# Loading two tokens of a head side by side, and splitting them by token parity, in a gated linear attention + MLP kernel

## The chip, the cores and the metric

The kernel runs on one core of one Trainium2 chip. The metric is the device time of one execution in microseconds; several runs without a profile give a median. One further execution is recorded by the hardware profiler; the views quoted below are of that execution. TensorE appears in them as PE (matmuls) and PEld (weight loads), VectorE as DVE, ScalarE as ACT, GpSimd as POOL, SyncE as SP. A `q` after an engine's name means its queue of instructions, where DMAs are issued.

## The reference

Four tensors `q`, `k`, `v`, `f_logit` of shape (4 batches, 8 heads, 768 tokens, 48) go through a gated recurrence for each batch and head, and the result, laid out as (4, 768, 384), goes through a LayerNorm and a two-layer MLP with a residual:

```python
f = 1 / (1 + exp(-f_logit))
for t in range(S):
    state = f[:, :, t, :, None] * state + einsum('bhd,bhe->bhde', k[:, :, t], v[:, :, t])
    y[:, :, t] = einsum('bhd,bhde->bhe', q[:, :, t], state)
x = y.transpose(0, 2, 1, 3).reshape(B, S, H * D)
xn = (x - mean) / sqrt(var + 1e-6) * g_ln
out = x + maximum(xn @ w_ch1, 0) @ w_ch2       # 384 -> 1536 -> 384
```

## The kernel before

The 768 tokens are cut into 12 units of 64 tokens, each of all four batches, so a unit is 256 rows of the MLP. `attention(n)` has the stages of unit n's recurrence (gates, two scans along the tokens, scores, values, state), and `mlp(n)` its two layers. From unit 3 on the first layer runs as 15 products of blocks (`by_blocks`, lines 916 to 979) and the second, from unit 2 on, as seven (`product` inside `mlp`, L1025). All matmuls are in float32.

The order of all work is written out by hand. `START` (lines 302 to 318) and `UNIT` (319 to 325) are lists of tokens that `run` (1075) turns into instructions: `a3.k` is the stage `k` of unit 3, `m2` the next step of unit 2's MLP, `l5k` a load of k for unit 5 from SP's queue and `L5k` from ACT's, `p4q0` the split number 0 of q for unit 4 with its write on POOL's queue and `P4q1` number 1 with its write on SP's, `x4k` the transpose of k for unit 4, which SP issues. Each engine and each queue works through its instructions in this order, so an instruction that waits holds what stands behind it. The transposes, the output and most of the loads share SP's queue.

For the recurrence, f, q and k are needed with the feature of a head on the partitions and the tokens along the free dimension, while DRAM has them with the features innermost. Units 0 to 2 (`n < DIRECT`) are transposed by TensorE in `across` (646). Units 3 to 11 go another way[...]:

- `load` (455) fills a tile `[128, G, H, 64]` (G = 2, H = 8). Batch b of a unit has 64 tokens; they lie on the partitions (b % 2) * 64 to + 64, in the half g = b // 2 of the tile. Each token of a head is 48 floats, 192 B, followed by 16 columns of filling. One load is one batch: 64 partitions x 8 heads, 512 runs of 192 B. Four loads make one tensor of a unit.
- `split` (425) takes one half g of the tile (two batches) and has ACT copy it into a tile `planes` that holds the low and the high 2-byte words apart (L433). There are two such buffers, used in turn by all tensors. Then a DMA writes `planes` into a DRAM tile (L437), 256 runs of 1 KB.
- `transfer` and `transposed` (439, 449) turn both halves in one DMA transpose (L452) of 256 rows by 1,024 two-byte columns, 8 blocks of 128 columns. Low and high words of a value land side by side, so the tile can be read as float32: `turned` for f and q, `qraw` for k.

From unit 3 on, q is loaded into the raw tile of k (`raw_of`, 414), which shows as `kraw<-in_q_dram` in the profile. The gated key `kh` goes the same way once more, with the name K: it is split (`Kplanes`), written and transposed into `kt` (stage `kt`, 768), which the state update uses.

In `attention`, a pair of heads of one of the two halves g is numbered by e, 0 to 7; `pairs` (617) lists them with g outermost. `do_kept` (721) scales the state by the unit's total gates, `do_values` (782) copies the result of the recurrence out of PSUM into `x`.

The filling is 40.0 for f, so that its gate is 1, and 0.0 for q and k (401 to 403). The smallest product of gates is kept in `least`, and at the end a flag decides whether a slower path must redo the work (L1118 to L1128, 1132).

Of the kernel before, what the change touches and what calls it, by code (L numbers as in the profile page):

```python
# [12 lines left out]
U16 = mybir.dt.uint16  # L13
AF = mybir.ActivationFunctionType
ALU = mybir.AluOpType
# [313 lines left out]
def kernel(  # L329
# [38 lines left out]
    DIRECT = 3  # L368
    HALVED = 1
    PIECE = 768  # L370

    outer = ctx.enter_context(tc.tile_pool(name="outer", bufs=1))
    ident = outer.tile([P, P], FP32)
# [8 lines left out]
    raws = fast.enter_context(tc.tile_pool(name="raws", bufs=2))  # L382
# [11 lines left out]
    def one_bank(name):  # L394
        return ps1.tile([P, 512], FP32, tag="one", name=name)
# [2 lines left out]


    wide_heads = {}  # L400
    for name, fill in (("f", 40.0), ("q", 0.0), ("k", 0.0)):
        t = consts.tile([P, G, H, 64], FP32, name=f"{name}raw")
        nc.gpsimd.memset(t[:, :, :, D:64], fill)
        wide_heads[name] = t
    loaded = {}

# [13 lines left out]
    def whole(n, name):  # L420
        if name != "K":
            return raw_of(n, name)
        return by_gates[n].rearrange("p (g s) t -> p g s t", g=G)

    def split(n, name, g, queue):

        if n >= NU or n < DIRECT:
            return
        if (n, name) not in halved:
            halved[n, name] = drams.tile([P, 2, G, 64 * H], U16, tag=f"{name}halves",  # L430
                                         name=f"{name}halves{n}")
        planes = raws.tile([P, 2, 64 * H], U16, tag="planes", name=f"{name}planes{n}_{g}")
        nc.scalar.copy(  # L433
            out=planes,
            in_=whole(n, name)[:, g].rearrange("p h e -> p (h e)").bitcast(U16).rearrange(
                "p (c two) -> p two c", two=2))
        queue.dma_start(out=halved[n, name][:, :, g], in_=planes)  # L437

    def transfer(n, name):

        if n >= NU or n < DIRECT:
            return
        if not turned:
            turned["k"] = wide_heads["q"].rearrange("p g h e -> p (g h e)").rearrange(
                "p (s t) -> p s t", t=T)
            turned["f"] = turned["q"] = work.tile([P, NS, T], FP32, name="turned")
        transposed(turned[name].rearrange("p (g s) t -> p g (s t)", g=G), n, name)

    def transposed(dst, n, name):
        there = halved.pop((n, name))  # L450
        to = dst.rearrange("p g c -> p (g c)").bitcast(U16)
        nc.sync.dma_start_transpose(out=to.rearrange("p (a r) -> p a r", a=GA),  # L452
                                    in_=there.rearrange("p two g c -> (p two) (g c)"))

    def load(n, name, gs=range(B // 2), engines=(nc.sync,)):
        if n >= NU:
            return
        if name != "v":
            loaded[n, name] = raw_of(n, name)
        elif (n, name) not in loaded:  # L460
            loaded[n, name] = raws.tile([P, G, H, D], FP32, tag="rawv", name=f"v{n}")
        src = {"f": f_logit, "k": k, "q": q, "v": v}[name]
        for b in (b for b in range(B) if b // 2 in gs):
            engines[b % len(engines)].dma_start(  # L464
                out=loaded[n, name][(b % 2) * T:(b % 2 + 1) * T, b // 2, :, 0:D],
                in_=src[b, :, n * T:(n + 1) * T, :].rearrange("h p d -> p h d"))

    load(0, "f", (0,), (nc.sync, nc.scalar))

    power = consts.tile([P, 2], FP32)  # L470
# [24 lines left out]
    state = consts.tile([P, 2, GA, D], FP32)  # L495
# [118 lines left out]

    pairs = [(g, a) for g in range(G) for a in range(NP)]
# [8 lines left out]
    def attention(n):  # L626

        both = range(G)
        gt = gates
# [13 lines left out]
        def of(gs):  # L643
            return [ega for ega in enumerate(pairs) if ega[1][0] in gs]
# [75 lines left out]

        def do_kept():

            if n:
                nc.vector.tensor_tensor(
                    out=new("kept", [P, 2, GA, D]), in0=state, op=ALU.mult,
                    in1=at["total"].rearrange("p (e b) -> p b e", b=2).unsqueeze(3).broadcast_to(
                        [P, 2, GA, D]))

        def do_carried():

# [37 lines left out]
        def do_kt():  # L768

            kt, kh = new("kt", [P, GA, P]), at["kh"]  # L770
            if n >= DIRECT:
                transposed(kt.rearrange("p (g a) c -> p g (a c)", g=G), n, "K")
                return
            for g in range(G):
                pt = one_bank(f"kp{n}").rearrange("p (a c) -> p a c", a=NP)
                for a in range(NP):
                    e = g * NP + a
                    nc.tensor.transpose(
                        pt[:, a], kh[:, 2 * e:2 * e + 2].rearrange("p b t -> p (b t)"), ident)
                nc.scalar.copy(out=kt[:, g * NP:(g + 1) * NP], in_=pt)  # L780

        def do_values(gs=both):
            py, sc, vt = at["py"], at["sc"], loaded[n, "v"]
            for e, (g, a) in of(gs):
# [12 lines left out]
            for b in range(2):  # L797
                nc.scalar.copy(out=xv[half(b), 1, gsl], in_=pyv[half(1 - b), 1, gsl])
# [276 lines left out]
    def run(plan):  # L1075
        for token in plan.split():
            kind, rest = token[0], token[1:]
            if kind == "a":
# [3 lines left out]
                if "a" + n not in running:  # L1082
                    running["a" + n] = attention(int(n))
# [32 lines left out]
    for m in range(3, NU):  # L1116
        run(UNIT.format(m=m, n=m + 1, o=m + 2, p=m + 3, z=m + 4))
        if m == NU - 3:  # L1118
            worst = consts.tile([P, 1], FP32)
            nc.vector.tensor_reduce(out=worst, in_=least, axis=mybir.AxisListType.X, op=ALU.min)  # L1120
        if m == NU - 2:
            pw = one_bank("pw")
            nc.tensor.transpose(pw[0:1, 0:P], worst, ident)
            least_one = consts.tile([1, 1], FP32)
            nc.vector.tensor_reduce(out=least_one, in_=pw[0:1, 0:P], axis=mybir.AxisListType.X,
                                    op=ALU.min)
            nc.vector.tensor_scalar(out=small, in0=least_one, scalar1=LEAST, scalar2=None,
                                    op0=ALU.is_lt)  # L1128
# [37 lines left out]
```

## Time and profile before

| What | us |
|---|---|
| median of 3 runs without a profile | 442.06 (441.48 to 442.35) |
| the profiled execution, its own time | 445.22 |
| its span, first to last instruction | 443.2 |
| DVE, ACT, POOL busy | 332.1, 215.5, 111.2 |

The span is 2.0 us shorter than the profiled execution's own time. In the middle of the run a unit takes about 33 us: the second-layer products of units 6, 7, 8 and 9 begin at 231.95, 266.22, 300.29 and 333.22 us. In the profile's names, L464 is any load, L433 a copy of a split, L437 its write, L452 a transpose, L1038 the output; a line is that of the helper, so it is the tile's name that tells which tensor is meant. A matmul's end is modelled, and a wait for several semaphores is put down to the one that came last.

### The profile page before, as it was taken

The page shows a single profiled execution, that of the slowest core. Times are in us where ns is not written, and L with a number is a line of the kernel's source. Part 1 is how long each engine was busy: PE and PEld are TensorE (multiplying, and loading weights), DVE is VectorE, ACT ScalarE, POOL GpSimd, SP SyncE. Part 2 cuts the span into 40 slices and gives each one's busy share as a digit, 9 for nine tenths or more (in the row PEclk, how much of TensorE's full clock was granted, in tenths as well). Part 3 has the DMA queues.
Part 4 walks back from the last instruction along what each step waited for, and adds up shares of the span by engine and source line. Part 5 has one row for each costly group of instructions (what it writes and reads, how often), then busy time and mean ns, then how long its engine had stood idle before and what let it go on. Part 6 is the DMA issues. An engine that isn't in the chain of part 4 may idle for free.

```text
span 443.2 us, 12936 instructions
## 1 busy us (share of the span) xinstructions
PE 422.5 (95%) x5435; PEld 392.0 (88%) x5435; DVE 332.1 (75%) x538; ACT 215.5 (49%) x364; POOL 111.2 (25%) x136
## 2 busy tenths in 40 slices
PE   6889998999999999999989999998999999999995
PEld 4678885667889999989979999989999999999995
DVE  5998676578856888788777798787798798567361
ACT  2665655444543573663554465456366443160320
POOL 2352334831023115014013114014114003002011
PEclk9999999999999999999998999999999999999999
DMA  9999898987897896899798798799787780400101
GB/s 166 274 232 226 173 229 215 190 150 192 163 206 170 210 202 169 164 186 200 161 187 197 176 188 176 188 174 201 179 184 188 180 157 10 123 1 10 29 5 36
DMA packets 200270, 71.68 MB, mean 162 GB/s; under 512 B 179408, under 2 KB 194000, under 8 KB 200208
## 3 DMA queue, kind: packets, MB, share of 16 engines
q1 hardware_dynamic: 176992, 57.27, 64.5%
q0 software_dynamic: 2960, 9.70, 6.3%
q10 hardware_dynamic: 20256, 3.84, 5.5%
q8 instruction: 44, 0.72, 0.7%
q14 instruction: 18, 0.15, 0.1%
HBM read 28.31 MB, written 23.59 MB: 117 GB/s over the span
## 4 chain that ended last, share of the span: by engine, by line
PE 64%; SPq 12%; DMA 11%; ACT 5%; issue 5%; DVE 1%; POOL 1%; ACTq 0%; POOLq 0%; DVEq 0%
PE pp L1025 28%; PE po L1006 7%; PE bx L931 7%; DMA kraw<-in_k_dram 6%; SPq L464 6%; PE by L931 5%; SPq L1038 3%; PE ph L996 2%; DMA qraw<-in_q_dram 2%; PE py L738 2%; PE ph L880 2%; PE bv L931 2%; PE shared L752 2%; PE bz L931 2%; PE bw L931 2%
## 5 line engine op out<-in xcount | busy, mean ns | idle before, releaser
L1025 PE MATMUL pp<-w,h 128*128 128x192 f32 x240 | 43.0, 337 | 5.1 <-ACT h L942 5.0
L1025 PEld LDWEIGHTS pp<-w,h 128*128 128x128 f32 x240 | 40.5, 196 | 6.2 <-ACT h L942 6.0
L942 ACT ACTIVATE h<-h 128x512 f32<-128x512 f32 x45 | 27.7, 627 | 35.6 <-DVE h L939 29.5
L1025 PE MATMUL pp<-mixed,h 128*128 128x192 f32 x240 | 42.3, 326 | 0.0
L1025 PE MATMUL pp<-mixed,s 128*128 128x192 f32 x240 | 40.6, 326 | 0.0
L1025 PEld LDWEIGHTS pp<-mixed,h 128*128 128x128 f32 x240 | 39.6, 190 | 0.3
L1025 PEld LDWEIGHTS pp<-mixed,s 128*128 128x128 f32 x240 | 39.3, 190 | 0.0
L433 ACT COPY kplanes<-kraw 128x1024 uint16<-128x1024 uint16 x18 | 18.9, 1051 | 32.4 <-DMA kraw<-in_k_dram 20.1
L1006 PE MATMUL po<-w,h 128*128 128x384 f32 x96 | 32.5, 490 | 1.8 <-ACT h L998 1.8
L658 DVE TENSOR_TENSOR_SCAN after<-gates,ends 128x1040 f32<-128x1040 f32 (+1 forms) x13 | 29.8, 2291 | 3.1 <-ACT gates L689 3.1
L433 ACT COPY Kplanes<-kh 128x1024 uint16<-128x1024 uint16 x18 | 18.3, 1050 | 28.3 <-DVE kh L706 16.5
L996 PE MATMUL ph<-xt,w 128*128 128x256 f32 x144 | 31.9, 381 | 0.0
L996 PEld LDWEIGHTS ph<-xt,w 128*128 128x128 f32 x144 | 27.2, 190 | 4.3 <-ACT xt L868 0.2
L939 DVE TENSOR_TENSOR h<-h,by 128x512 f32<-128x512 f32 x36 | 24.7, 687 | 8.0 <-PE by L931 3.2
L1006 PEld LDWEIGHTS po<-w,h 128*128 128x128 f32 x96 | 17.8, 190 | 13.3 <-issue 2.2
L931 PE MATMUL bx<-y,v 128*128 128x128 f32 x216 | 29.4, 279 | 0.0
L670 DVE TENSOR_TENSOR_SCAN upto<-gates,starts 128x1040 f32<-128x1040 f32 (+1 forms) x13 | 28.1, 2158 | 0.5
L1033 POOL TENSOR_TENSOR p1x<-p,x 128x192 f32<-128x192 f32 x10 | 10.7, 1066 | 67.0 <-ACT p L1040 67.0
L931 PEld LDWEIGHTS bx<-y,v 128*128 128x128 f32 x216 | 26.2, 192 | 0.5
L758 DVE TENSOR_TENSOR sc<-shared,causal 128x1024 f32<-128x1024 f32 x11 | 13.5, 1224 | 15.1 <-PE shared L752 15.1
L939 DVE TENSOR_TENSOR h<-h,bx 128x512 f32<-128x512 f32 x27 | 18.3, 677 | 8.4 <-PE bx L931 8.4
L813 POOL TENSOR_SCALAR rstd<-mv 128x2 f32<-128x2 f32 (+1 forms) x13 | 3.3, 250 | 82.6 <-DVE mv L811 82.4
(169 smaller groups left out, 952.9 us busy)
## 6 DMA issues: line engine op xcount, KB each, us to landing
w_0words<-in_moe_w_ch_dram SPq DMA_DIRECT2D x7, 768.0 KB, 6.4
v<-in_v_dram SPq DMA_DIRECT2D x46, 96.0 KB, 4.2
kraw<-in_k_dram SPq DMA_DIRECT2D x40, 96.0 KB, 4.4
fhalves<-fplanes SPq DMA_DIRECT2D x14, 256.0 KB, 2.6
khalves<-kplanes POOLq DMA_DIRECT2D x14, 256.0 KB, 4.7
kraw<-in_q_dram SPq DMA_DIRECT2D x36, 96.0 KB, 3.3
fraw<-in_f_logit_dram ACTq DMA_DIRECT2D x27, 96.0 KB, 3.6
Khalves<-Kplanes POOLq DMA_DIRECT2D x10, 256.0 KB, 3.4
```

The lines of the kernel that those rows point to most:

```text
L433: nc.scalar.copy(out=planes, in_=whole(n, name)[:, g].rearrange("p h e -> p (h e)").bitcast(U16).rearrange("p (c two) -> p two c", two=2))
L464: engines[b % len(engines)].dma_start(out=loaded[n, name][(b % 2) * T:(b % 2 + 1) * T, b // 2, :, 0:D], in_=src[b, :, n * T:(n + 1) * T, : ...
L658: nc.vector.tensor_tensor_scan(out=at["after"].rearrange(flat)[:, c0:c1][:, ::-1], data0=gt[:, c0 + 1:c1 + 1][:, ::-1], data1=ends.rearran ...
L670: nc.vector.tensor_tensor_scan(out=at["upto"].rearrange(flat)[:, c0:c1], data0=gt[:, c0:c1], data1=starts.rearrange(flat)[:, c0:c1], initi ...
L758: nc.vector.tensor_tensor(out=sc.rearrange("s r e t -> s (r e) t"), in0=at["ps"].rearrange("s r e t -> s (r e) t"), in1=causal.unsqueeze(1 ...
L931: nc.tensor.matmul(banks[bank][:, i], lhsT=right[:, i * P:(i + 1) * P], rhs=left, start=new and i == 0, stop=True, skip_group_check=True)
L939: nc.vector.tensor_tensor(out=out[to], in0=out[to], in1=bank, op=op)
L942: nc.scalar.activation(out=out[to], in_=out[to] if bank is None else bank, func=AF.Relu)
L996: nc.tensor.matmul(ph[:, j], lhsT=w1[:, m, (i + j) * P:(i + j + 1) * P], rhs=xt[:, m], start=m == 0, stop=m == KD - 1)
L1006: nc.tensor.matmul(po, lhsT=h[:, i, g * P:(g + 1) * P], rhs=w2[:, i], start=i == 0, stop=i == KF - 1)
L1025: nc.tensor.matmul(pp, lhsT=a[:, i], rhs=b[:, i], start=i == 0, stop=i == KH - 1)
L1038: engine.dma_start(out=out[2 * g + b, n * T:(n + 1) * T, cols], in_=o[half(b)])
```

## The change

From unit 3 on, a load puts two neighbouring tokens of a head side by side on one partition (R = 2). Batch b now lies on the partitions b * 32 to + 32, and a partition holds 8 heads x 96 floats without filling: one load has 256 runs of 384 B. A split takes the tokens of one parity i of all four batches: for each head 64 floats from column h * 96 + i * 48, so the 16 columns after the 48 are those of a neighbouring token or head instead of filling. The two parities are the two halves in the DRAM tile, whose runs become 2 KB, and the transpose of f, q and k has 512 rows and 4 blocks of 128 columns. K keeps its own shape.

With that the segments of a unit come out in another order, heads outside and batches inside (`by_heads`), so the state is reordered once, in `do_kept` of unit 3, and the copies to `x` read PSUM in the new order. The filling of f is 0.0, and the last minimum is taken over the 48 real rows of each 64 only. Units 0 to 2, `START` and `UNIT` stay as they are.

```diff
@@ def split @@
-            halved[n, name] = drams.tile([P, 2, G, 64 * H], U16, tag=f"{name}halves",
+            halved[n, name] = drams.tile([P, 2, 2, 64 * H], U16, tag=f"{name}halves",
...
-        nc.scalar.copy(
-            out=planes,
-            in_=whole(n, name)[:, g].rearrange("p h e -> p (h e)").bitcast(U16).rearrange(
-                "p (c two) -> p two c", two=2))
-        queue.dma_start(out=halved[n, name][:, :, g], in_=planes)
+        if name == "K":
+            src = by_gates[n].rearrange("p (i s) t -> p i (s t)", i=2)[:, i].bitcast(U16).rearrange(
+                "p (c two) -> p two c", two=2)
+            to, there = planes, halved[n, name][:, :, i]
+        else:
+            src = raw_of(n, name).rearrange("p g h e -> p (g h e)")[
+                :, i * D:i * D + (H - 1) * R * D + 64]
+            src = bass.AP(tensor=src.tensor, offset=src.offset,
+                          ap=[src.ap[0], [R * D, H], [1, 64]]).bitcast(U16).rearrange(
+                              "p h (c two) -> p two h c", two=2)
+            to, there = planes.rearrange("p two (h c) -> p two h c", h=H), halved[n, name][:, i]
+        nc.scalar.copy(out=to, in_=src)
+        queue.dma_start(out=there, in_=planes)
@@ def transfer, transposed @@
-        transposed(turned[name].rearrange("p (g s) t -> p g (s t)", g=G), n, name)
+        transposed(turned[name].rearrange("p s t -> p (s t)"), NP,
+                   halved.pop((n, name)).rearrange("p i two c -> (p i two) c"))
...
+    def transposed(dst, blocks, there):
+        nc.sync.dma_start_transpose(
+            out=dst.bitcast(U16).rearrange("p (a r) -> p a r", a=blocks), in_=there)
@@ def load @@
-            engines[b % len(engines)].dma_start(
-                out=loaded[n, name][(b % 2) * T:(b % 2 + 1) * T, b // 2, :, 0:D],
-                in_=src[b, :, n * T:(n + 1) * T, :].rearrange("h p d -> p h d"))
+            to = loaded[n, name]
+            if name == "v" or n < DIRECT:
+                to = to[(b % 2) * T:(b % 2 + 1) * T, b // 2, :, 0:D]
+                rows = src[b, :, n * T:(n + 1) * T, :].rearrange("h p d -> p h d")
+            else:
+                to = to.rearrange("p g h e -> p (g h e)")[
+                    b * T // R:(b + 1) * T // R, 0:H * R * D].rearrange("p (h c) -> p h c", h=H)
+                rows = src[b, :, n * T:(n + 1) * T, :].rearrange("h (p i) d -> p h (i d)", i=R)
+            engines[b % len(engines)].dma_start(out=to, in_=rows)
@@ def do_kept @@
+            for b in range(2):
                 nc.vector.tensor_tensor(
-                    out=new("kept", [P, 2, GA, D]), in0=state, op=ALU.mult,
...
+                    out=kept[:, b].rearrange("p (a g) d -> p a g d", g=G),
+                    in0=state[:, b].rearrange("p (g a) d -> p a g d", g=G), op=ALU.mult,
...
@@ def do_values @@
-            pyv = py[:, :, 0:GA * D].rearrange("t r (g a d) -> t r g a d", g=G, d=D)
+            pyv = py[:, :, 0:GA * D].rearrange(f"t r ({order} d) -> t r g a d", g=G, d=D)
```

More of the change, by code (lines that the diff above doesn't have):

```diff
@@ L370 @@
     PIECE = 768
+    R = 2
     outer = ctx.enter_context(tc.tile_pool(name="outer", bufs=1))
@@ L400 @@
     wide_heads = {}
-    for name, fill in (("f", 40.0), ("q", 0.0), ("k", 0.0)):
+    for name in "fqk":
         t = consts.tile([P, G, H, 64], FP32, name=f"{name}raw")
-        nc.gpsimd.memset(t[:, :, :, D:64], fill)
+        nc.gpsimd.memset(t[:, :, :, D:64], 0.0)
         wide_heads[name] = t
@@ L418, with split @@
     by_gates = {}
[L420 to L425, printed above, removed]
+    def split(n, name, i, queue):
         if n >= NU or n < DIRECT:
@@ L429, in split @@
         if (n, name) not in halved:
-            halved[n, name] = drams.tile([P, 2, G, 64 * H], U16, tag=f"{name}halves",
+            halved[n, name] = drams.tile([P, 2, 2, 64 * H], U16, tag=f"{name}halves",
                                          name=f"{name}halves{n}")
-        planes = raws.tile([P, 2, 64 * H], U16, tag="planes", name=f"{name}planes{n}_{g}")
-        nc.scalar.copy(
-            out=planes,
-            in_=whole(n, name)[:, g].rearrange("p h e -> p (h e)").bitcast(U16).rearrange(
-                "p (c two) -> p two c", two=2))
-        queue.dma_start(out=halved[n, name][:, :, g], in_=planes)
+        planes = raws.tile([P, 2, 64 * H], U16, tag="planes", name=f"{name}planes{n}_{i}")
+        if name == "K":
[11 more added lines that the diff above has]
+        queue.dma_start(out=there, in_=planes)
     def transfer(n, name):
@@ L446, in transfer @@
             turned["f"] = turned["q"] = work.tile([P, NS, T], FP32, name="turned")
-        transposed(turned[name].rearrange("p (g s) t -> p g (s t)", g=G), n, name)
[L449 to L453, printed above, removed]
+        transposed(turned[name].rearrange("p s t -> p (s t)"), NP,
[3 more added lines that the diff above has]
+            out=dst.bitcast(U16).rearrange("p (a r) -> p a r", a=blocks), in_=there)
     def load(n, name, gs=range(B // 2), engines=(nc.sync,)):
@@ L613, in mix_step @@
         late["steps"].send(engine)
-    pairs = [(g, a) for g in range(G) for a in range(NP)]
+    by_batch = [(g, a) for g in range(G) for a in range(NP)]
+    by_heads = [(g, a) for a in range(NP) for g in range(G)]
     x_of, norm_of, xn_of, xt_of, y_of, h_of, sums_of = {}, {}, {}, {}, {}, {}, {}
@@ L628, in attention @@
         both = range(G)
+        pairs, order = (by_batch, "g a") if n < DIRECT else (by_heads, "a g")
         gt = gates
@@ L721, in do_kept @@
         def do_kept():
-            if n:
+            if not n:
+                return
+            kept = new("kept", [P, 2, GA, D])
+            by = at["total"].rearrange("p (e b) -> p b e", b=2)
+            if n != DIRECT:
+                nc.vector.tensor_tensor(out=kept, in0=state, op=ALU.mult,
+                                        in1=by.unsqueeze(3).broadcast_to([P, 2, GA, D]))
+                return
+            for b in range(2):
                 nc.vector.tensor_tensor(
-                    out=new("kept", [P, 2, GA, D]), in0=state, op=ALU.mult,
-                    in1=at["total"].rearrange("p (e b) -> p b e", b=2).unsqueeze(3).broadcast_to(
-                        [P, 2, GA, D]))
+                    out=kept[:, b].rearrange("p (a g) d -> p a g d", g=G),
+                    in0=state[:, b].rearrange("p (g a) d -> p a g d", g=G), op=ALU.mult,
+                    in1=by[:, b].rearrange("p (a g) -> p a g", g=G).unsqueeze(3).broadcast_to(
+                        [P, NP, G, D]))
         def do_carried():
@@ L771, in do_kt @@
             if n >= DIRECT:
-                transposed(kt.rearrange("p (g a) c -> p g (a c)", g=G), n, "K")
+                transposed(kt.rearrange("p e c -> p (e c)"), GA,
+                           halved.pop((n, "K")).rearrange("p two i c -> (p two) (i c)"))
                 return
@@ L1123 @@
             nc.tensor.transpose(pw[0:1, 0:P], worst, ident)
+            of_heads = pw[0:1, 0:P].rearrange("o (r e) -> o r e", r=2)[:, :, 0:D]
             least_one = consts.tile([1, 1], FP32)
-            nc.vector.tensor_reduce(out=least_one, in_=pw[0:1, 0:P], axis=mybir.AxisListType.X,
+            nc.vector.tensor_reduce(out=least_one, in_=of_heads, axis=mybir.AxisListType.XY,
                                     op=ALU.min)
```

## The prediction, made before the changed kernel was run

> **What bounds the kernel now.** I began with the page: the engine shares, then the slices.
>
> ```profile
> span 443.2 us, 12936 instructions
> PE 422.5 (95%) x5435; PEld 392.0 (88%) x5435; DVE 332.1 (75%) x538; ACT 215.5 (49%) x364; POOL 111.2 (25%) x136
> DMA  9999898987897896899798798799787780400101
> ```
>
> TensorE is busy for 422.5 of 443.2 us. The change takes no matmul away, so all that it can win lies in the 20.7 us of TensorE's idle time. The third line says that the DMA engines are nearly full until late in the run. Next, the table of waits, of which these are the lines that touch the change:
>
> ```profile
> ACT kplanes L433 <- DMA kraw<-in_k_dram: 20.1, 8, 4.4
> ACT gates L685 <- DMA turned<-fhalves: 11.3, 6, 2.7
> ACT qplanes L433 <- DMA Khalves<-Kplanes: 7.6, 5, 2.2
> PE pp L1025 <- ACT h L942: 5.0, 4, 2.0
> ACT qplanes L433 <- DMA kraw<-in_q_dram: 2.2, 2, 1.1
> PE po L1006 <- ACT h L998: 1.8, 1, 1.8
> PE shared L825 <- DMA kt<-Khalves: 0.9, 1, 0.9
> ```
>
> Columns: total us, times, longest. Only the three PE lines cost time directly: 5.0 + 1.8 + 0.9 = 7.7 us. The first, four stalls, comes from ACT's order. The timeline by engine of one such stall (SP, then ACT, then PE; start, duration, what, and in brackets the idle time before and its cause):
>
> ```profile
> 221.30 1.08 SPq L437 DMA_DIRECT2D qhalves<-qplanes  x1
> 222.43 3.56 SPq L464 DMA_DIRECT2D kraw<-in_k_dram  x4
> ...
> 229.32 1.05 ACT L433 COPY kplanes<-kraw 128x1024 uint16<-128x1024 uint16 x1 [4.03 <-DMA kraw<-in_k_dram]
> 230.27 1.14 ACT L942 ACTIVATE h<-h 128x512 f32<-128x512 f32 x2
> ...
> 231.95 2.48 PE L1025 MATMUL pp<-w,h 128*128 128x192 f32 x7 [2.05 <-ACT h L942]
> ```
>
> Four loads of k are issued over 3.56 us, the last lands 3.2 us later (225.99 to 229.2), ACT sits in front of the copy for 4.03 us, the two Relus queue behind it, and the first matmul of the second MLP product waits 2.05 us. The same picture stands at 197.32 (1.02 us), 300.29 (1.63) and 333.22 (0.35): together 5.05 us.
>
> In the chain of waits the queue of SP is on the path too (SPq 12%, DMA 11%): between 174 and 191 us it issues without a real pause, and steps that take 0.57 us elsewhere take 1.05 (L437 at 186.99), four loads 3.46 instead of 2.63 to 2.78. I read those stretches as a queue that is held back by the backlog of descriptors. Last, the DMA queues:
>
> ```profile
> q1 hardware_dynamic: 176992, 57.27, 64.5%
> q0 software_dynamic: 2960, 9.70, 6.3%
> q10 hardware_dynamic: 20256, 3.84, 5.5%
> ```
>
> q10 is ACT's queue. Its packets can be counted: 37 loads (27 f, 8 k, 2 v) of 512 runs of 192 B = 18,944, of 20,256. They took 5.5% of 16 x 443.2 = 390 us, so 19.3 ns each. q0 (POOL's 37 writes of 256 KB, 64 packets of 4 KB and 16 small ones each) took 447 us, about 185 ns for 4 KB or 46 ns for 1 KB.
>
> **What the Trainium skill says.** *DMA: Bandwidth & Descriptors*, "Specifications", gives 512 B as the least size for full rate; the trace agrees in kind: 192 B in 19.3 ns is 10 B/ns, 4 KB in 185 ns is 22 B/ns. The same page, "How a descriptor splits into AXI transactions", says that a read that starts off a 256 B boundary fetches from the boundary below. Rows of 192 B then cost 6, 12, 10 and 8 beats in turn, 36 for four tokens; runs of 384 B cost 12 and 16, 28. This is an estimate from the page; no view shows beats. "Issuing engines are not separate DMA queues" on that page: moving a load between queues saves no engine time. Here q1, q10 and q0 do fill the same 16 engines. *ScalarE: Activation LUTs*, "What ACT_TABLE_LOAD costs", prices an instruction with immediate operands at 186 ns and 0.833 ns per element of a lane, whatever the function; 186 + 853 = 1.04 us for 1024 elements, and the trace has 1.04 us for the copies of all four tensors.
>
> **The change, part by part.** (1) Loads. For units 3 to 11, 9 x 3 x 4 = 108 loads have 256 runs of 384 B for 512 of 192 B: 27,648 packets less. A 384 B packet is in no row. Bounds: 19.3 ns (size free) and 38.5 ns (size everything, nothing saved). The line through 192 B and 1 KB gives 19.3 + 192 x (46 - 19.3)/832 = 25.5 ns, which I take. One load then needs 256 x 25.5 = 6,530 instead of 9,880 engine-ns, 0.21 us less on 16 engines (bounds 0 and 0.31); four loads 0.84 us, the twelve of a unit 2.5 us in about 34.
>
> (2) Writes of the halves for f, q, k: 2 KB runs for 1 KB on the SP queue (27 of them, 128 packets less each). By the same line 2 KB costs about 90 ns against 2 x 46: nothing, at most a tenth of a us each.
>
> (3) Splits. Same count and size of copies on ACT, now with rows of 64 instead of one run of 512. I take 1.04 us as before (bounds: no reason for less; if each row cost 10 ns more, 0.16 us each, hidden except where ACT is late). But each split now needs all four loads, and not the two of its half. For k in the steady part nothing changes: k1 is split first, and its half came with the last two loads. For q it does: q0 is split first, and its two loads were the early ones. What is queued behind q0 on ACT is q1, and q1 has another wait, for the buffer that the K write frees: it started 0.99, 1.62, 2.07 and 2.16 us after q0's end (at 184.05, 218.32, 286.31, 320.83). So q0 may be late by that much and nothing moves. Its last load is issued until 180.03 in the first of these units and may land 2.97 us later. With (1) I expect 2.2 to 2.6. Hidden. At 62.12 (first split of k, unit 3) and 89.64 (unit 4) two more loads are awaited too; half the packets pay for them.
>
> (4) Transposes of f, q, k as 512 rows x 4 blocks instead of 256 x 8. The count of packets in q1 leaves 2,064 per transpose, so 2,048 of 256 B: the same in both shapes. SP is held 1.3 to 4.4 us now, by backlog I think. I take no change of their own; bounds -0.5 and +1 us each. ACT's gates wait for f in six units, but the copies after them have 0 to 2.8 us of idle time and four PSUM banks in front of TensorE, so +1 us stays hidden.
>
> (5) DVE: the scaling of the state in unit 3 in two halves instead of one of 0.95 us; about 0.1 us once, on an engine with idle time. Memsets, the last minimum, the copies out of PSUM in another order: nothing.
>
> **The sum.** How much sooner does k come? The four issues shrink from 3.46-3.65 to about 2.7 us (0.8 to 0.9), their own packets drain 0.84 us sooner, and the stretched steps ahead (L1038, L437, about 0.5 us) shrink in part: 1.6 to 2.2 us. That removes 1.02, 1.63 and 0.35 whole and about 1.8 of 2.05: 4.8 us. In units without a stall (249 to 266 us) TensorE is busy for all 17.00 us, so the next limit is TensorE. The wait of 0.9 for kt (two transposes of 3.50 and 4.35 us behind loads of f and k) goes: 0.85. The wait of 1.84 at 72.18 comes from the second k split at 68.91, behind the write of fplanes and a backlog of loads and weights; two tensors' loads are 8 x 0.21 = 1.7 us less engine time. I take 1.0. Together 6.65 us; I leave 0.6 for stalls that come back smaller. So about -6.05. Against the profiled execution: 445.22 (span 443.2 and 2.0 around it) to 439.2. The median of the runs without a profile is 442.06, 3.2 lower; I assume the same stalls there: **436.0 us**.
>
> **Rivals.** *Most of the price is bytes.* If 384 B costs near 38 ns, only the issues shrink (256 KB writes with 256 runs take 0.57, loads with 512 take 0.65: 0.3 us per four) and some backlog: 0.5 us in four stalls, 2 us: 440.0. For it: GB/s in the slices stays at 150 to 250. Against: 19.3 ns for 192 B.
> *Nothing:* what the loads give, waits on planes buffers and on SP's order take; 442. Against: the k copies wait on no buffer in the four stalls.
> *Slower: the wait for the fourth q load.* If loads land no sooner, the last after 3.67 us as k's did at 293.89, q0 ends 0.7 us after q1 could have started in all four units (180.03 + 3.67 = 183.70 against 183.00; 0.7 each in the others). q1, its write on SP and the loads of k behind that slip by as much, and four stalls grow by 0.7: 442.06 + 2.9 = 445. It decides from 2.97 us between issue and landing. For it: ACT waited for q already in two units, with only two loads awaited. Against: fewer packets, and unstretched issues.
>
> **Chances and range.** Forecast (434.5 to 438.5) 0.63; mostly bytes 0.15; nothing 0.05; slower 0.17. Changes under 0.2%, 0.9 us, can't be told from none. Faster 0.78, same 0.05, slower 0.17. The range ends at the full 7.7 us with a little for the clock (434.0) and at 442.0, where the slower case is left out.
>
> **What would show it.** Right: about 169,200 packets in all (200,270 - 27,648 - 3,456), DMA share lower in the middle slices, four k loads in about 2.7 us on SP, ACT's wait for k under 10 us of 20.1, PE's for L942 under 1 us, q0 later but q1 still behind the K write. Wrong: transposes that take longer on SP; the q0 copy ending after the K write lands; or PE's idle time gone while the span stays, which would mean a lower clock or longer matmuls. What would make me wrong is above all a landing time that hangs on something other than packets.

## The result, and the profile after

| | before | after |
|---|---|---|
| median of 20 runs each, us | 442.1 (440.89 to 445.24) | 445.65 (441.52 to 452.74) |
| the profiled execution, us | 445.22 | 446.89 |
| its span, us | 443.2 | 444.9 |
| first block product (`bw`) of unit 3, the first full unit, us | 145.2 | 152.1 |
| the same of unit 11, eight units later, us | 410.9 | 412.6 |

The changed kernel is slower: ratio 1.0063, 95% interval 1.0038 to 1.0088, where 436.0 us had been forecast. (Ratios leave disturbed runs out, medians keep them, so the two can differ by a few tenths of a per cent.)

The last two rows of the table say where to look. (The expectations below call the first of these marks the second-layer product of the first full unit. The second-layer products begin with unit 2's at 127.95, so the one at 231.95 us is that of unit 5, and the four starts listed in "Time and profile before" belong to units 5 to 8.) Eight full units take 265.7 us before and 260.5 after: there the change gains 5.2 in these two executions. What comes ahead of the first full unit takes 6.9 us longer. A gain and a larger loss, in different stages. First the page of the changed kernel: granted clock and DMA share in slices, and ACT's queue.

```profile
PEclk9999999779999999999999999999999999999999
DMA  9999897662798887997989987897896790400101
...
q10 hardware_dynamic: 12064, 3.84, 4.3%
```

Two digits of the granted clock fall to 7: slices of 11 us, the eighth and ninth, from 78 to 100 us. In the same slices the DMA engines are at 6 and 6, where before has 9 and 8. Then the waits (total us, times, longest).

```profile
ACT kplanes L440 <- DMA kraw<-in_k_dram: 9.4, 6, 3.0
...
PE kp L799 <- DVE x L1032: 4.2, 1, 4.2
...
ACT gates L696 <- DMA turned<-fhalves: 3.0, 5, 1.4
```

TensorE's four waits for ACT in front of the second layer (5.0 us before) have no line left, and ACT's wait for k fell from 20.1 to 9.4, that for f (gates) from 11.3 to 3.0. New is one wait of TensorE for DVE, 4.2 us at one place. The timeline of TensorE (start, duration, what, and in brackets the idle time before) shows what follows from it:

```profile
69.56 10.84 PE L1027 MATMUL po<-w,h 128*128 128x384 f32 x32
84.59 1.97 PE L799 MATMUL kp<-ident,kh 128*128 128x128 f32 x8 [4.19 <-DVE x L1032]
...
89.10 4.93 PE L1027 MATMUL po<-w,h 128*128 128x384 f32 x8
93.96 1.15 PE L758 MATMUL py<-kept,qh 48*64 48x48 f32 x64
```

The wait of 1.84 us in front of the 32 `po` matmuls is gone: they begin at 69.56, not 72.18. But the `kp` behind them, which here waits for the PSUM bank that DVE's addition (L1032) frees, begins 2.0 us later than before (84.59, not 82.57), and then eight `kp` take 1.97 us for 1.04 and eight `po` 4.93 for 2.84. In the kernel before, `kp` began ahead of that addition (PE, then DVE):

```profile
82.57 1.04 PE L778 MATMUL kp<-ident,kh 128*128 128x128 f32 x8
```

```profile
79.58 0.17 DVE L667 TENSOR_SCALAR total<-after 128x16 f32<-128x16 f32 x1
...
80.06 2.33 DVE L670 TENSOR_TENSOR_SCAN upto<-gates,starts 128x1040 f32<-128x1040 f32 x1
82.77 0.55 DVE L1011 TENSOR_TENSOR x<-x,po 128x384 f32<-128x384 f32 x1 [0.38 <-PE po L1006]
```

So it cannot have waited for it; there the transposes of q (`tr`), which come after `kp`, are what the addition holds, as the waits of e9 below show. `kp` stands behind the addition in the changed kernel, e1, e2, e3, e6 and e7, and does not in the kernel before, e4, e5 and e8 to e12. The order of the work is the same in both kernels, so this is a side effect of the change; its cause stays open.

For the slow matmuls the windows say why (each engine's busy time, TensorE's first; the last three columns are the granted clock, the DMA share and GB/s):

```profile
82.00:84.00 2.00, 0.00 (x0) 0.00 (x0) 2.00 (x1) 0.00 (x0) 2.00 (x1) 0.81 0.62 233
84.00:92.00 8.00, 6.63 (x21) 5.02 (x22) 3.43 (x6) 3.17 (x4) 6.28 (x5) 0.50 0.48 105
```

After the gap TensorE runs at half clock for some 9 us; the clock is already down in the last stretch of the gap (0.81 granted from 82 to 84). That is the clock gate of the Trainium skill (*TensorE: Matmul & The Clock Gate*, "HAM oscillation — how this bites in real kernels", which warns of gaps above about 3.4 us); 4.19 us is beyond that.

So by `py` the changed kernel is 6.9 us behind (93.96 against 87.11). In parts: `kp` later, 2.0; from `kp` to `py` 9.4 us against 4.5. The runs below in which `kp` stands behind the addition and the clock stays full (e2, e3, e6, e7) take 5.5: so 1.0 goes with that order, in which half of the transposes of q wait 0.8 us for DVE, and 3.9 with the clock.

Why is DVE late at 84? Its timeline:

```profile
79.43 1.45 DVE L678 TENSOR_SCALAR total<-after 128x16 f32<-128x16 f32 x1
...
81.20 2.88 DVE L681 TENSOR_TENSOR_SCAN upto<-gates,starts 128x1040 f32<-128x1040 f32 x1
84.01 0.52 DVE L1032 TENSOR_TENSOR x<-x,po 128x384 f32<-128x384 f32 x1
```

In front of these stands `v`, at 78.82. Before, `v` ran at 78.97, `total` took 0.17 us and the scan 2.33. DVE is as early as before up to `v`; `total` and the scan then take 1.83 us longer. They run beside POOL's `mixed`, which begins at 79.83 and began at 81.32 before, since q is split earlier. ACT does that split (at 76.96, before at 78.42) after it has issued unit 4's four loads of f, and the new loads hold its queue for less time (the first line is before, the second after):

```profile
74.63 2.78 ACTq L464 DMA_DIRECT2D fraw<-in_f_logit_dram  x4
74.10 1.85 ACTq L475 DMA_DIRECT2D fraw<-in_f_logit_dram  x4
```

The Trainium skill (*SBUF — State Buffer*, "Who interferes with whom") says that the two engines share a port pair. Of an instruction of DVE in a two-port mode and one of GpSimd, the first takes the pair for its whole length and the other waits; one of DVE with two inputs in SBUF contends with one of GpSimd that reads SBUF. The times fit that in the main: the first `mixed` ends at 80.83, `total` at 80.88, and before, where the scan came first, the scan kept its 2.33 us and `mixed` took 1.86 for 1.00. But `total` began 0.40 us ahead of `mixed`, while POOL was issuing the write of q's split (79.25 to 79.81), and what held it then no view shows.

And why is `v` not earlier, with smaller loads? The chain of waits of the changed kernel (start, duration, what) leads back to the loads:

```profile
55.67 7.19 DMA kraw<-in_k_dram
...
63.91 0.93 ACT w_0upper L547
...
79.52 1.38 DVE total L678
...
84.59 1.97 PE kp L799 x8
```

The first split of k for unit 3 waits until 62.96; ACT's unpacking of a block of weights, `w_0upper`, stands behind it, and DVE and POOL finish that block. In the kernel before it was 62.12 and 63.07. Yet SP issued these four loads 2.0 us earlier. The two answers for `kraw` in that window (for how long SP is held, least, median and most in ns, then the first and last start in us):

```profile
L464 SPq DMA_DIRECT2D kraw<-in_k_dram x4: 596/617/1134, 55.9 to 57.9; - x4
...
DMA to landing us min/median/max: 4.7/5.3/5.9
```

```profile
L475 SPq DMA_DIRECT2D kraw<-in_k_dram x4: 312/378/450, 53.9 to 55.7; - x4
...
DMA to landing us min/median/max: 7.1/7.2/7.5
```

The first is before, the second after: issued from 53.9 instead of 55.9, they take 7.1 to 7.5 us to land instead of 4.7 to 5.9. The last lands at 62.9, and before at 62.6. Half the packets bought nothing here.

For the steady part, the stall that the prediction showed (2.05 us at 231.95) in the changed kernel; SP, then ACT:

```profile
227.86 3.21 SPq L475 DMA_DIRECT2D kraw<-in_k_dram  x4
...
233.61 1.05 ACT L440 COPY kplanes<-kraw 128x1024 uint16<-128x1024 uint16 x1 [1.67 <-DMA kraw<-in_k_dram]
234.56 1.15 ACT L963 ACTIVATE h<-h 128x512 f32<-128x512 f32 x2
```

The wait in front of the copy is 1.67 us for 4.03, and the Relus behind it stop nobody: the second layer of this unit has no wait.

### The profile page after: what moved, and what is told of

Same layout as the page of the kernel before. It is cut to its first block, busy times and chain, and to the rows that moved or that the text cites. A ratio compares the mean times of both kernels' runs of the same rounds, so it can differ in the third digit from the quotient of the medians.

```text
span 444.9 us, 12945 instructions
## 1 busy us (share of the span) xinstructions
PE 423.7 (95%) x5435; PEld 390.9 (88%) x5435; DVE 335.5 (75%) x539; ACT 216.2 (49%) x364; POOL 111.0 (25%) x136
## 3 DMA queue, kind: packets, MB, share of 16 engines
q10 hardware_dynamic: 12064, 3.84, 4.3%
## 4 chain that ended last, share of the span: by engine, by line
PE 80%; DMA 11%; DVE 3%; ACT 2%; issue 1%; SPq 1%; POOL 0%; ACTq 0%; DVEq 0%; POOLq 0%
PE pp L1046 31%; PE bx L952 12%; PE by L952 9%; PE po L1027 5%; PE bz L952 4%; PE py L808 3%; PE py L758 3%; PE ph L901 3%; PE shared L772 2%; DMA kt<-Khalves 2%; DMA qraw<-in_q_dram 2%; PE ph L1017 2%; PE bv L952 2%; PE bw L952 2%; PE shared L846 2%; DMA kraw<-in_k_dram 2%
## 5 line engine op out<-in xcount | busy, mean ns | idle before, releaser
L1046 PE MATMUL pp<-w,h 128*128 128x192 f32 x240 | 41.4, 329 | 0.8
L1046 PEld LDWEIGHTS pp<-w,h 128*128 128x128 f32 x240 | 38.7, 190 | 2.2 <-DVE h L998 2.2
L1027 PE MATMUL po<-w,h 128*128 128x384 f32 x96 | 34.8, 515 | 0.1
L1027 PEld LDWEIGHTS po<-w,h 128*128 128x128 f32 x96 | 18.8, 202 | 12.7 <-issue 2.0
```

The source lines that it names most:

```text
L1027: nc.tensor.matmul(po, lhsT=h[:, i, g * P:(g + 1) * P], rhs=w2[:, i], start=i == 0, stop=i == KF - 1)
L1046: nc.tensor.matmul(pp, lhsT=a[:, i], rhs=b[:, i], start=i == 0, stop=i == KH - 1)
```

## The experiments

The theory, A1 in the expectations: the loss is made in the start-up, by ACT's first split of k for unit 3, which now waits for all four loads and holds the unpacking of weights behind it, while TensorE runs ahead; the gap that results brings the half clock. Its rivals are told in the expectations themselves: a gap or a clock that comes by chance, the order on DVE alone, the new layout's cost in the steady units, later a late unpacking that does harm only when TensorE is ahead. Each kernel was timed beside the kernel before on the same chip: 440.81 us (49 runs) for the first four, 440.12 (67 runs) for the next four, 443.63 (43 runs) for e9 and e10, 442.84 (21 runs) for the last two.

**e1, the changed kernel again.** No edit.

> The changed kernel once more, for a second profile. Theory A (the steady units gained what was forecast, the start-up lost more): the four waits for L942's h stay gone, and in the start-up TensorE again sits idle for over 3 us before the transposes of kh of unit 2 and then runs at half clock for some 9 us; 444 to 447 us where that happens, and a profile without the half clock would be about 4 us shorter. Theory B (the new loads, splits or transposes cost something in every unit): no half clock need show, and a unit takes longer than the 32.9 us of before.

445.12 us, ratio 1.0068 (1.0039 to 1.0098). The profile repeats the gap at the same place: `kp` waits 4.08 us, `total` 1.46, the scan 2.88, half clock from 84.8 to 91.6. The expectation is met, and the gap isn't chance. The half clock isn't in every execution, though: four of these twenty runs have a mean granted clock of 0.996 or more, which leaves no room for 7 us at half (an estimate: that alone takes 0.008 off the mean), and they took 440.3 to 443.8 us.

**e2 and e5, the scan first.** DVE's order around the gap, in the changed kernel:

```diff
-P3q0 u a2.upto m0 m1 m0 a2.kept ...
+P3q0 a2.upto u m0 m1 m0 a2.kept ...
```

> The changed kernel with two neighbouring steps of the start-up exchanged: the scan upto of unit 2 stands ahead of one mixing step on DVE, so that it runs in DVE's idle time and not beside POOL's mixing, and the addition that frees the PSUM bank comes sooner. Theory A: the idle time before the transposes of kh shrinks from 4.2 to under 1 us, the clock stays full, 436.5 to 439 us (ratio to before 0.988 to 0.993). Theory B: the start-up is not where it is lost; 444 us or more.

441.93 us, ratio 1.0025 (1.0000 to 1.0049): 3.2 us less than the changed kernel beside it by the medians, 1.9 by the ratios, whose intervals overlap a little. That is short of the 436.5 to 439 expected. `kp` waits 1.60 us, not under 1, and the clock stays full from 80 to 95. DVE's timeline shows that the collision moved rather than went: the scan takes 3.68 us, now beside POOL's last unpacking (79.55 to 81.36), and `v` 1.41.

```profile
79.87 3.68 DVE L681 TENSOR_TENSOR_SCAN upto<-gates,starts 128x1040 f32<-128x1040 f32 x1
83.47 1.41 DVE L612 TENSOR_TENSOR v<-w 128x512 f32<-128x512 f32 x1
84.80 0.54 DVE L1032 TENSOR_TENSOR x<-x,po 128x384 f32<-128x384 f32 x1
```

This whole timeline stands 3.8 us later than the others, for a half clock at 26 to 33 us; the addition follows 11.5 us after the first `po`, where it was 14.5 in the changed kernel. The same exchange in the kernel before is the control:

> The kernel before with the same exchange of upto and one mixing step as in the run upto_first. In the profile of before the addition that frees the bank came as soon as TensorE's products ended, so with theory A the exchange takes nothing away here: within 1.5 us of before. If it gains 3 us here as well, the exchange is worth something by itself and says nothing of the change.

441.86 us, ratio 1.0020 (0.9994 to 1.0046): 1.7 us above before by the medians, 0.9 by the ratio. By itself the exchange gains nothing, so what it gains in the changed kernel is part of what the change lost there.

**e3, the gap filled.** Eight matmuls whose result nobody reads, ahead of stage `kt` of unit 2, to keep TensorE busy:

```diff
-... a2.kept p3q1 a2.kt a2.q m0 ...
+... a2.kept p3q1 b b b b b b b b a2.kt a2.q m0 ...
+    def busy():
+        nc.tensor.matmul(shared[:, 0, 0:2 * P], lhsT=ident,
+                         rhs=ident.unsqueeze(1).broadcast_to([P, 2, P]), start=True, stop=True)
```

> The changed kernel with eight matmuls without use put in front of the transposes of kh of unit 2, to keep TensorE busy in the idle time and nothing else. Theory A: the transposes start no sooner (about 84.6 us), but the clock stays full and the 4 to 5 us that half clock costs go: 440 to 442 us. If the clock isn't the price, 444 us or more, as with theory B.

448.27 us, ratio 1.0187 (1.0145 to 1.0229): slower still. By the expectation 444 us or more would mean that the clock isn't the price, but the profile says otherwise. That profile, which at 445.43 us is the fastest of its six runs, shows what was wanted, full clock and `po` x8 in 2.75 us:

```profile
84.35 1.09 PE L803 MATMUL kp<-ident,kh 128*128 128x128 f32 x8 [0.76 <-DVE x L1036]
```

`py` begins at 89.8 instead of 94.0, and `kp` to `py` takes 5.5 us instead of 9.4, so the clock is worth 3.9 us at that point. In that execution TensorE then loses 2.08 us at 131, in a wait that the profile names "issue", and others: unit 3's `bw` begins at 149.9, only 2.2 us ahead of the changed kernel. Why its other runs are slower than the profiled one stays open; this run prices the clock in one execution and settles nothing about the whole time.

**e4, the new layout from unit 6 on.** Units 3 to 5 loaded, split and transposed as before:

```diff
+    SIDE = 6
-            if name == "v" or n < DIRECT:
+            if name == "v" or n < SIDE:
...
-        pairs, order = (by_batch, "g a") if n < DIRECT else (by_heads, "a g")
+        pairs, order = (by_batch, "g a") if n < SIDE else (by_heads, "a g")
```

> The new layout from unit 6 on alone; units 3 to 5, which the start-up loads, keep the old one. Theory A: the start-up takes as long as before, the late units lose their waits for k: three or four of the four waits of 5.0 us in all gone, 437 to 440 us. Theory B: 442 us or more, since six of nine units still have the new layout.

439.6 us, ratio 0.9995 (0.9965 to 1.0025). The start-up is that of before (`po` 72.2, `py` 87.2, first full unit 145.4), the waits for ACT in the second layer are gone, the last unit stands at 406.4 instead of 410.9. So the loss of 6.9 belongs to units 3 to 5. The time is within the 437 to 440 expected, but beside the kernel before it is no gain: the interval runs from 0.35% faster to 0.25% slower, with six of nine units in the new layout.

**e7, from unit 4 on**, the same with `SIDE = 4`, so that unit 3 alone is as before:

> The new layout from unit 4 on, unit 3 alone with the old one. If unit 3's loads and splits are what upsets the start-up (theory A, both forms): as the run from unit 6, 438 to 441 us, no idle time over 3 us near 80 us. If the loads of units 4 and 5, which the start-up issues too, share in it: 442 us or more.

441.62 us, ratio 1.0040 (1.0015 to 1.0066); 147.1 at the first full unit. The split of unit 3 is at 61.76, the scan takes 2.33 again, `kp` waits 0.65, no half clock after the first 20 us: of the 6.9 us some 5 are back with unit 3 alone. Of the other 1.9, `py` at 88.3 is 1.2 late, and 0.9 of that is again the 5.5 us from `kp` to `py`, since `kp` stands behind the addition here too. At 128 TensorE waits 1.7 us; the profile puts that down to DVE, and the landing of `kt`, 9.1 us after its issue at 119.12, fits as well. The time lies between the two expectations, 441 and 442.

**e6 and e8, the split behind the unpacking.** The changed kernel, with the split moved past one fetch, one unpacking and a2.after in the list:

```diff
-m1 p3k0 f w a2.after r a2.k P3k1 ...
+m1 f w a2.after r p3k0 a2.k P3k1 ...
```

> The changed kernel with the first split of k of unit 3, which now waits for all four loads, moved behind one step that unpacks a piece of the weights on ACT. Theory A1 (the wait for the fourth load holds the unpacking on ACT, and with it DVE and POOL): the unpacking starts at about 61 us, not 63.9, DVE's addition comes 2 us sooner, the idle time falls to 2 us or less without half clock, 438 to 441 us. Theory A2 (the wait matters little; what counts is that TensorE comes sooner and that POOL's mixing gets in front of DVE's scan): still over 3 us idle, 444 us or more.

440.06 us, ratio 1.0011 (0.9985 to 1.0037), as A1 expected. The changed kernel had 445.12 and 1.0068 on another chip, so that the move is worth 5.1 us by the medians, less the 0.7 by which the chips differ, and 2.5 us (0.57%) by the ratios. `w_0upper` runs at 60.76 (63.91), and DVE, then TensorE, show:

```profile
76.61 0.17 DVE L678 TENSOR_SCALAR total<-after 128x16 f32<-128x16 f32 x1
...
77.10 2.32 DVE L681 TENSOR_TENSOR_SCAN upto<-gates,starts 128x1040 f32<-128x1040 f32 x1
80.95 0.55 DVE L1032 TENSOR_TENSOR x<-x,po 128x384 f32<-128x384 f32 x1 [1.52 <-PE po L1027]
```

```profile
81.56 1.09 PE L799 MATMUL kp<-ident,kh 128*128 128x128 f32 x8 [0.65 <-DVE x L1032]
```

The addition waits for TensorE again (1.52 us), and only its own length stands in front of `kp`. `mixed` begins at 78.50, when `total` is done. No half clock (eight `po` take 2.75 us), and the first full unit is at 144.5, where the changed kernel had 152.1. But the move takes more away than the change added: `total` comes 2.8 us sooner than in the changed kernel and 3.0 sooner than in the kernel before. The control, the same move in the kernel before:

> The kernel before with the same move of the first split of k of unit 3. It waited 1.5 us there for two loads. Theory A1: unpacking about 1 us sooner, 439 to 441.5 us beside 441 to 442; theory A2: within 1 us of before.

441.33 us, ratio 1.0035 (1.0012 to 1.0058). Its profile is early (143.5), its runs aren't: alone, the move gains nothing, and by the ratio it costs 0.1 to 0.6%, where A1 expected a small gain.

**e9 and e12, only the later load awaited.** The kernel before, its halves of k for unit 3 exchanged, so that the half loaded last is split first:

```diff
-m1 p3k0 f w a2.after r a2.k P3k1 w l3q ...
+m1 p3k1 f w a2.after r a2.k P3k0 w l3q ...
```

> The kernel before, with the two halves of k of unit 3 exchanged in the order of START: the half whose loads were issued last is split first. So the first split waits for the fourth load, as it does in the changed kernel, and nothing else is changed; its loads keep 512 runs of 192 B. Theory A1 (the wait for the fourth load holds the weight unpacking behind it on ACT, and that is enough): first split at 63 to 64 instead of 62.12, the wait of TensorE for ACT h behind the second split stays or shrinks, DVE's addition that frees the bank comes 1 us or more later, kp waits 2 us or more, the second-layer product of the first full unit begins at 147 to 152 instead of 145.2, ratio 1.004 to 1.01. Theory A3 (the late unpacking costs only because TensorE runs ahead with the smaller loads, so that it idles for over 4 us and the clock drops): without the smaller loads TensorE still stalls at 72 and is not ahead, kp waits under 2 us, no half clock at 80 to 95, ratio 0.998 to 1.003. Theory B (the late unpacking doesn't matter): ratio 1.0 and the marks within 0.5 us of before.

444.34 us beside 443.63; ratio 1.0048 (1.0022 to 1.0075), though the medians of all runs differ by only 0.7. The ratio is the one that A1 expected; the marks are not. The split is at 62.35, TensorE is ahead all the same (`po` at 69.77), `kp` follows at 80.09 without a wait, and the transposes of q behind it wait twice for little; the clock stays full, and `py` begins at 87.12 as before:

```profile
82.19 0.66 PE L650 MATMUL tr<-ident,qraw 128*128 128x128 f32 x4 [1.06 <-DVE x L1011]
83.95 0.66 PE L650 MATMUL tr<-ident,qraw 128*128 128x128 f32 x4 [1.11 <-DVE qh L677]
```

`total` takes 0.17 and the scan 2.33 here, with POOL's `mixed` from 80.30 on. ACT is held for 2.81 us by the issue of f's loads, so POOL's write and `mixed` come 1.0 us later behind `v` than in the changed kernel, and `total` is done before them. A second execution:

> One more look at the kernel before with the halves of k of unit 3 exchanged. Its median was 0.5% above before while its profile showed no loss against the profile of before. If that loss is of the same kind as the change's (theory A1), an execution should show waits of kp and tr for DVE of 3 us or more, or a half clock at 80 to 95, and the second layer at 147 or later. If the profile is again like before's (145 to 146), the loss of its median stays open.

441.87 us, beside a median of 442.84 for before; split at 61.52, `py` at 86.3, first full unit at 144.1, no half clock. What the runs of e9 lost stays open.

These two runs correct A1. Counted from ACT's previous unpacking, so that the executions can be laid side by side, the first split of k begins after

| first split waits for | executions | us after the unpacking before it |
|---|---|---|
| two loads of 192 B runs | before, e4, e5, e7 | 6.17, 6.02, 6.64, 6.06 |
| the last of four, 192 B runs | e9, e12 | 6.73, 6.82 |
| all four, 384 B runs | after, e1, e2, e3 | 7.58, 7.32, 7.53, 7.29 |

By the means (6.22, 6.78, 7.43), waiting for the fourth load explains about half of the 1.2 us; with 6.64 so close to 6.73 that rests on few executions. The other half are loads that take longer to land: 6.5 to 7.2 us in the median of four in the last row, 4.0 to 5.8 in the others. (In e10 and e11 below, runs of 192 B took 6.7 and 5.9 us too.)

The lateness reaches DVE whole: in the five executions in which TensorE is ahead, this split comes first on ACT and DVE's order is that of the list (after, e1, e3, e9, e12), `v` begins 15.9 us after the first split (15.86 to 15.93). But lateness and a TensorE that is ahead don't suffice for the gap of 4 us. In the changed kernel POOL comes sooner as well, and its collision adds the last 1.8; and the whole wait stands in front of `kp`, where e9 and e12 have `kp` done first. An estimate: with the first split 6.17 us after the unpacking, as before, `v` would come 1.4 us sooner, at 77.4, and `total` would be over before POOL's write begins at 79.25. No run makes that change alone.

**e10 and e11, the best of both.** The new layout from unit 6 on, and the split behind the unpacking:

```diff
+    SIDE = 6
-m1 p3k0 f w a2.after r a2.k P3k1 ...
+m1 f w a2.after r p3k0 a2.k P3k1 ...
```

> The new layout from unit 6 on alone, and the first split of k of unit 3 two tokens later, behind the first weight unpacking. This is the order and the layout that the earlier runs favour. Theory A1 (the loss of the change is all in the start-up; the gain is all in the steady units): start-up as in the kernel before with the move (first full unit at 143.5), steady units without waits for ACT h, the last unit's second layer at 403 to 405, 437.5 to 439 us, ratio 0.993 to 0.998. Rival (the gain of the steady units is given back to the clock or the tail, as the first run from unit 6 on suggests): 440, ratio 0.999 to 1.002.

> The kernel of the run before (new layout from unit 6 on, first split of k of unit 3 behind the unpacking) once more, to settle whether it beats the kernel before. Theory (the gain of the steady units, 4 us, stands when the start-up is left alone): ratio 0.994 to 0.998, and an interval below 1. Rival (the start-up move costs in the runs what the units gain): 0.999 to 1.002. Its last profile had the wait for ACT h at 72 us back, 2.49 us, where the kernel before with the same move had none; if that wait comes and goes between executions, it may be gone here, and the first full unit then begins at 143 to 144 instead of 145.7.

The same kernel twice. 441.15 beside 443.63 us, ratio 0.9977 (0.9953 to 1.0002), and in the repeat, on another chip, 439.46 beside 442.84, ratio 0.9927 (0.9902 to 0.9951). All 16 runs of the repeat lie between 438.20 and 440.85. This version beats the kernel before in the repeat, by 2.2 to 4.3 us; the first time its interval just reached 1. The changed kernel wasn't timed beside it. The two intervals of the same kernel don't meet: on two chips its ratios are 0.5% apart. That is as much as the 0.57% between e1 and e6, which were timed on two chips as well. The changed kernel's two ratios, 1.0063 and 1.0068, agree, which speaks for e6's gain, but it is less firm than its interval says.

The wait for `h` at 72 us is there in both profiles (2.49 and 1.34), while e8, with the same move, had 0.46; A1's 143.5 for the first full unit wasn't met: 145.7 and 144.8. From there the repeat needs 260.3 us for eight units. The profiles don't show where the gain of the runs lies: e8, the same move with the old layout throughout, needs 261.4 for them and has a span of 437.2 us, the repeat 437.5.

## Why the prediction was wrong

- **What bounds the kernel.** Right in kind for the full units: the waits for ACT go. But the 5.0 us are those of one execution (see the sum), and the start-up has another limit.
- **(1) Loads.** The packets are as counted: 169,167. The price of 384 B was near, by an estimate: q10's share of 4.3% of 16 x 444.9 us is 306 us. Of its 12,064 packets 8,192 are of 384 B (32 loads); the other 3,872 (five loads as before, and 1,312 that were there before) at 19.3 ns take 75. That leaves 28 ns for each of 384 B; 25.5 was taken. That packets set the landing was wrong in the start-up: there 7.2 us stand against 5.3.
- **(2) Writes.** Taken at nothing. In the median they hold SP for 0.37 us for f and k and 0.53 for q, where it was 0.58 and 0.76. No run tests what that is worth.
- **(3) Splits. The step that failed.** "At 62.12 (first split of k, unit 3) and 89.64 (unit 4) two more loads are awaited too; half the packets pay for them." They didn't: the first split of k came at 62.96, 0.8 us later, and 1.4 us later against the unpacking before it. SP is held less, so it passes the block of 768 KB of weights to the DMA engines sooner (that issue takes 0.39 us for 2.16), and k goes in 2 us earlier but behind the same bytes. The Trainium skill (*DMA: Bandwidth & Descriptors*, "Queues, rings and completion order") says that on each DMA engine descriptors are consumed in ring order. No view shows the rings, but the landings fit: what was a held queue became a longer landing. The working named what stands behind the q split, q1, and never what stands behind this k split: the unpacking, on which DVE and POOL hang. Nor did it ask what smaller loads do on ACT's own queue: the issue of f's loads took 1.85 us for 2.78, and that helped to bring POOL into DVE's way. What the runs showed in place of a gain in the start-up is a loss of 6.9 us: TensorE idle for 4.19 us in front of `kp`, and 3.9 us lost to the half clock after it. The copies themselves are right, 1.04 us, and q stayed hidden: ACT's waits for it are 2.4 us in sum.
- **(4) Transposes.** Taken as unchanged. In the median SP was held 2.2 us for k, 2.7 for q, 2.6 for kt, where it had been 3.0, 3.1 and 1.8. That f came no later held: ACT's wait for it went from 11.3 to 3.0.
- **(5) DVE.** The split scaling is off the path; one instruction more. But "an engine with idle time" hid that at 82.77 DVE's addition had 0.38 us to spare against TensorE.
- **The sum.** The 4.8 us for four stalls were too many. All four are gone, and eight units gain 5.2, but some 1.7 of that are a half-clock stretch at 232 to 236 us that only before's execution had. In the four other executions with the old layout throughout (e5, e8, e9, e12) eight units take 261.4 to 263.7 us, not 265.7, and the second layer's waits for `h` come to 1.8 to 2.7 us, not 5.0. In the nine with the new layout in the full units they take 260.0 to 261.2. By the means of these two groups the full units gain about 1.7 us (an estimate from executions that differ in their start-up). "I assume the same stalls there" carried the stalls of an execution 3.2 us above the median over to the median. The 0.85 for kt didn't come: TensorE's wait for it is 1.2 us, 0.9 before. The "1.0" for the wait at 72.18 was taken whole on TensorE, 1.84, and was worth less than nothing: what is late next is the addition that frees the bank, and `kp`, which had not waited for it, now did. The sum asked that question for the full units and not for the start-up.
- **The rivals.** The slower one had the right kind, a split that waits for its fourth load, but laid it on q in the full units, 0.7 us in each of four, and that its 445 came out close to the median is luck. The kind of wait was in the text; its place was not looked for where ACT carries something others need.

What is shown: the loss is in units 3 to 5 (e4), most of it in unit 3 (e7); with the unpacking ahead of the split (e6) or DVE's order changed (e2) the gap is below 2 us, the clock stays up and much of the loss is back, and neither gains in the kernel before. What is argued: that the split's later start alone makes DVE late, since e6 moves more than that, and e9, which makes the split late in the old layout, has no gap; that the 768 KB in front are what lengthens the landing, since no run moved that load; and how much of the loss comes from `kp` standing behind the addition, which no run took away alone.

## What to carry to other kernels

Fewer and larger packets made an issue shorter, but here an issue that came 2.0 us earlier, behind a large transfer, only waited longer. When a copy starts to wait for more loads, look at what stands behind it on its engine in every stage, not only in the steady one. And when a stall of the bounding engine goes, find its next releaser and that one's slack: here 0.38 us on DVE, and a gap of 4.2 us cost 3.9 more in clock. Price stalls from more than one execution: one profile had 5.0 us of them, four others 1.8 to 2.7.

## What the runs showed of the hardware

- Half clock came with a gap of 4.1 to 4.2 us and lasted 7 to 10 us (two executions); gaps of 1.60 (e2), 1.84 (before), 2.49 (e10) and 2.63 us (e5) in this stage brought none. Yet before had about 3.4 us of it at 232 after a gap of 2.05 us, and e2 as much at 132 after one of 1.96, both shorter than the 3.4 us of the Trainium skill's page cited above. Nine of the fourteen profiles here have a stretch of it in their first 20 us, of 3.4 (e4, e8), 6.8 or 10.2 us (e2), which the others lack.
- The collision of DVE and POOL cost a small instruction the most for its size, and who began first matters: `total`, 128x16, took 0.17 us alone and 1.45 beside POOL's write issue and `mixed`; the scan took 2.33 us where it began ahead of `mixed` (before, e9), 2.88 where it began behind (after) and 3.68 behind an unpacking (e2); a `mixed` took 1.00 alone and 3.02 behind the scan.
- A load of q with 256 runs of 384 B held SP for 0.48 us in the median (0.31 to 0.72), one with 512 runs of 192 B for 0.64 (0.60 to 2.20), 36 loads each.
